# Moving batch 4's key-value product one unit later inside a hand-written order, and reordering tile 3 around it

## The chip, the cores and the metric

The kernel runs on one core of a Trainium2 chip. That core has a matrix engine (TensorE, PE in the profile, with its weight loads in a row of their own, PEld), a vector engine (VectorE, DVE), a scalar engine (ScalarE, ACT), a general engine (GpSimd, POOL) and a queue processor that issues most DMAs (SyncE, SP). Each engine works through its own instructions strictly in the order in which the program lists them, and waits on semaphores for what other engines have to deliver. The metric is the device time of one execution in microseconds; lower is better.

## The reference

Two things are computed one after the other, an efficient attention (softmax over the head dimension for the queries, over the sequence for the keys) and a two-layer network with a leaky ReLU:

```python
q_s = exp(q - max(q, axis=-1));  q_s /= sum(q_s, axis=-1)      # q, k, v: 8 x 8 x 576 x 64, float32
k_s = exp(k - max(k, axis=2));   k_s /= sum(k_s, axis=2)
kv  = einsum('bhsd,bhse->bhde', k_s, v)
x   = einsum('bhsd,bhde->bhse', q_s, kv)                       # then reshaped to 4608 x 512
h   = x @ w_in                                                 # 512 x 2048
out = maximum(0.01 * h, h) @ w_out                             # 2048 x 512 -> 4608 x 512
```

## The kernel before

Attention goes by batch (8 batches of 576 rows), the network by tile of 512 rows (9 tiles, numbered 0 to 8). The attention output is kept transposed in `xT`, which holds four batches and wraps round; tile 3 takes the last rows of batch 2 and the first 320 rows of batch 3, tile 4 the rest of batch 3 and the first 256 rows of batch 4. Matrix products run in bf16 with float32 sums. From tile 1 on the second layer, and from tile 5 on part of the first, is done with a seven-product scheme in place of eight (sums of blocks are formed on VectorE beforehand).

The order of the work is written out by hand. After the prologue, one long list of words, `SCORE`, is played word by word; each word emits a few instructions on one engine. So the list is at the same time the order of five in-order queues: where two words belong to different engines, only their dependencies bind them, and where they belong to one engine, the later one waits behind the earlier one. The words near the change, with `t` the tile and `b` the batch in the name:

- `tuij` is one unit of the first layer on TensorE: four matmuls of 128x512 into one PSUM bank (line 516; in tile 4, where the columns wrap round `xT`, eight of 128x256). A tile has 16 units, `u00` to `u07` and `u10` to `u17`. `tlij` is the leaky ReLU of that unit on ScalarE (line 525), which empties the bank into `gj`.
- `tPnsh` is a quarter of product `n` of the second layer on TensorE: four matmuls of 128x256 (line 947). Products 1, 6, 7 and 4 follow each other in one bank, 5 and 3 in a second, 2 in a third. `tn` are the block sums of `gj` on VectorE (`gs`, line 1004), on which products 5, 6, 7 and 3 depend. `tq1`, `tq5`, `tq6` and `tq21` copy a bank out on ScalarE before the next product goes on in it; `td11`, `td12` and `td22` are the closing sums on VectorE (line 896), and `tw` is the store of an output half, four DMAs on SP.
- For a batch `b`: `lk`, `lq`, `lv` load keys, queries and values (SP). `kt`, `km` and `ks` find the maximum of the keys and subtract it (VectorE; from batch 5 on the subtraction is on POOL, line 193); `ke` is their exponential (ScalarE, line 201) and `va`, `vb` cast the two halves of the values into `vb` (ScalarE, line 211). `kv` is the key-value product: 72 small matmuls on TensorE (line 294), into two PSUM banks for batch 4 and into the spare ends of two banks already taken for batches 5 to 7. `kr` (VectorE, line 326) and `kd` (ScalarE, line 332) divide it by the sum of the exponentials.
- `qm`, `qs`, `qe`, `qu`, `qn` are the softmax of the queries (VectorE, POOL line 256, ScalarE line 264, VectorE lines 273 to 275, VectorE line 280), and `qt` turns the result by a transposing DMA on SP into `qX` (line 457). `A` is the attention product of the turned queries on TensorE (line 438), `x` its copy into `xT` on ScalarE (line 429).
- `F` forms sums of `w_in` on VectorE that tile 5 needs (line 780), `X` sums of `xT`.

Buffers come from pools: six PSUM banks (`psB`) are shared by the first layer's units, product 2, the key-value product of batch 4 and the attention products (two banks each), two further banks (`psO`) by the other products. Six large buffers (`raw`) hold loaded keys, queries and values and later some sums. `vb` and `ke` exist once, so the casts and the exponential of batch 5 have to come after batch 4's key-value product has been computed; `gj` is a ring of five blocks.

What plays the list:

```python
def play(words, t=None):
    for word in words:
        if t is not None:
            of_tile(t, word)
        elif word[0].isdigit():
            of_tile(int(word[0]), word[1:])
        else:
            of_batch(word)
```

Of the kernel before, what the change touches and what calls it, by code (L numbers as in the profile page):

```python
# [25 lines left out]
def kernel(  # L26
# [17 lines left out]
    F2, O = moe_w_out.shape  # L44
# [741 lines left out]
    def xsums(t, steps=slice(0, 4)):  # L786
# [20 lines left out]
        qs3 qe3 2u14 2l14 2u02 2u06 2u12 lk5 2l05 2u13 2l02 2l06 2l12 km3 2u07 2u16 2u03 qu3 qn3 2l07 2l13  # L807
        2u17 1q21 2l03 2u15 2l15 2P100 ks3 ksB3 2n0_0 2l17 qs4 2P101 2P110 2P111 2P200 2l16 2P201 2P210
        2P211 2P500 2n0_1 2n1_0 2n1_1 2P501 2P510 lk4 kt4.0 lq5 ke3 kv3 kr3 2q1 2d11 2n2_0 1w0 2P600 qt3
        2P601 lv6 2P610 2P611 2P511 kd3 A3.0 kt4.1 2n2_1 2n3_0 kt4.2 2n3_1 A3.1 2q6 kt4.3 2q5 A3.2 2P700  # L810
        2P701 2P710 x3.01 2P711 x3.11 2d22 x3.10 2P300 x3.20 2P301 2P310 x3.21 qe4 km4 ks4 ksB4 kt5.0 lv4
        2P311 x3.00 2P400 va4 2P401 2P410 kt5.1 3u02 3l02 2P411 3u03 3u00 vb4 3l00 kt5.2 kt5.3 3u01 3l01 km5
        3l03 ke4 3u11 3l11 3u06 3u04 3l04 3u16 2q21 3l06 3l16 3u12 3l12 3u14 3u10 3l10 lk6 ks5 qu4 3u15 3l15
        kv4 3l14 kr4 kd4 3u07 2d12 qn4 3u05 3u13 3u17 3P100 3l05 3l07 3P101 3P110 3P111 lk7 3l13 3n0_0 3P500
        lv5 3l17 3n0_1 3P501 3P510 3q1 ke5 3n1_0 3n1_1 3n3_0 3P511 3P600 3n3_1 3q5 3P601 va5 3P610 3P611 3q6
        1w1 3P300 3P301 3P310 vb5 3P311 kt6.0 3n2_0 qt4 A4.0 A4.1 A4.2 kv5 x4.01 kt6.1 3n2_1 x4.00 x4.21
        x4.10 2w0 va6 3P700 kt6.2 kt6.3 3P701 3P710 qm5 qs5 3P711 3P200 3P201 x4.11 3P210 3P211 x4.20 kr5
        kd5 3d22 vb6 4u02 4l02 3P400 3P401 3d11 3P410 4u04 4u00 qe5 4l00 3P411 km6 4l04 4u05 4l05 3q21 4u03
        4u14 4l14 4l03 4u10 4l10 4u06 lv7 4u07 4u11 4l11 4u01 4l01 4l06 3d12 4l07 qu5 qn5 ks6 kt7.0 3w0 4u12
        4l12 4u13 F3 4l13 F1 4P100 4P101 4P110 F2 ke6 4u15 4P111 4q1 4n0_0 4l15 4u17 4l17 kt7.1 4n1_0 4u16  # L820
        3w1 4P500 4l16 4n0_1 4n2_0 qt5 A5.0 A5.1 x5.01 x5.10 x5.00 A5.2 kv6 x5.20 kt7.2 2w1 x5.11 4P501
        4P510 4n1_1 4P511 4q5 x5.21 4n3_0 4P600 4n3_1 4P200 4P601 4P610 4n2_1 X5.0 4P300 4P611 lq6 X5.1 X5.2
        4P201 4P301 4P310 4q6 X5.3 4P700 4P701 5u00 va7 kt7.3 4P210 F4 vb7 4P710 4P711 qm6 qs6 4d22 lq7 kr6
# [320 lines left out]
```

## Time and profile before

| | |
|---|---|
| median of 3 runs | 267.97 us (267.54 to 268.38) |
| the profiled execution | 267.58 us, of which the span of the instructions is 265.8 us |
| PE busy | 255.6 us (96%), 2570 instructions |
| DVE busy | 223.2 us (84%) |
| ACT busy | 193.7 us (73%) |
| POOL busy | 63.0 us (24%) |
| granted TensorE clock | 1.0 over the span |

A row of the chain or of a timeline gives start, duration and what ran, with `xN` for N instructions merged. In the chain of the work that ended last, "issue" is time for which the profile shows no cause. In the list of waits, a row says who waited for whom, for how long in total, how often, and the longest wait. A small share of matmul records can be missing from a trace, and the ends of matmuls are modelled. Tile 3's first layer runs from about 103 to 118 us, its second layer to about 134 us, tile 4's first layer from there to about 148 us.

### The profile page before, as it was taken

To read this page: it belongs to the slowest core of one execution; us is meant where nothing else is said; L and a number is where in the kernel's file an instruction comes from. 1 tells how busy PE (TensorE), PEld (TensorE's weight loads), DVE (VectorE), ACT (ScalarE), POOL (GpSimd) and SP (SyncE) were. 2 spreads that over 40 slices of the span, in tenths; PEclk is the share of its full clock that TensorE was granted. 3 is DMA by queue.
4 is the path that set the end of the run, shared out by engine and by line. 5 is a ranking of instruction groups with operands and counts; after the bars stand their busy time and mean duration, and the time that the engine had idled before them with its cause. 6 is when DMAs were issued, how large, how long until landed. Compare 5 with 4: busy or idle time off the path is not lost.

```text
span 265.8 us, 6314 instructions
## 1 busy us (share of the span) xinstructions
PE 255.6 (96%) x2570; PEld 190.1 (72%) x2582; DVE 223.2 (84%) x365; ACT 193.7 (73%) x370; POOL 63.0 (24%) x45
## 2 busy tenths in 40 slices
PE   8689999999999999999999999999999999999992
PEld 3267754457865687458888876688888888888882
DVE  2997899799998999989889896994998579679952
ACT  4977893699659769978887747887996489528930
POOL 2484442260038000250670019800000000000000
PEclk9999999999999999999999999999999999999999
DMA  7999999999898694858457725040382060042004
GB/s 241 344 210 357 317 210 273 337 310 294 250 397 298 149 327 143 289 221 176 174 129 155 225 72 170 18 91 4 85 176 68 21 139 2 0 97 63 1 2 158
DMA packets 37645, 46.48 MB, mean 175 GB/s; under 512 B 18160, under 2 KB 21232, under 8 KB 37616
## 3 DMA queue, kind: packets, MB, share of 16 engines
q1 hardware_dynamic: 32976, 36.64, 48.0%
q0 software_dynamic: 4320, 8.91, 13.4%
q10 hardware_dynamic: 320, 0.52, 0.6%
q8 instruction: 20, 0.33, 0.5%
q14 instruction: 9, 0.07, 0.1%
HBM read 36.70 MB, written 9.44 MB: 174 GB/s over the span
## 4 chain that ended last, share of the span: by engine, by line
PE 84%; DMA 6%; ACT 2%; DVE 1%; issue 1%; POOL 0%; ACTq 0%; POOLq 0%
PE acc L947 37%; PE ph L516 28%; PE ph L917 15%; DMA w_in_sb<-in_moe_w_in_dram 3%; DMA qX<-qe 3%; PE po L438 2%; PE pkv L294 1%; ACT ke L201 1%; PE po L294 1%; DVE k_raw L380 1%; PE pout L541 1%; ACT vb L211 1%; ACT qe L264 0%; POOL w_in_sb L129 0%; DVE out_sb L896 0%
## 5 line engine op out<-in xcount | busy, mean ns | idle before, releaser
L516 PE MATMUL ph<-xT,w_in_sb 128*128 128x256 bf16 (+3 forms) x488 | 83.6, 323 | 0.9 <-DMA w_in_sb<-in_moe_w_in_dram 0.2
L525 ACT ACTIVATE gj<-ph 128x512 bf16<-128x512 f32 (+2 forms) x113 | 59.1, 577 | 14.3 <-PE ph L516 11.1
L516 PEld LDWEIGHTS <-w_in_sb 128*128 128x128 bf16 x496 | 48.1, 98 | 29.6 <-DMA w_in_sb<-in_moe_w_in_dram 0.7
L947 PEld LDWEIGHTS <-gs 128*128 128x128 bf16 x512 | 49.5, 98 | 6.4 <-issue 0.2
L256 POOL TENSOR_TENSOR q_raw<-q_raw,qmax 128x2304 f32<-128x2304 f32 (+3 forms) x10 | 29.7, 2975 | 64.9 <-DVE qmax L225 64.9
L947 PEld LDWEIGHTS <-gj 128*128 128x128 bf16 x384 | 37.4, 98 | 6.8 <-issue 0.5
L947 PE MATMUL acc<-w_out_sb,gj 128*128 128x256 bf16 x256 | 32.4, 273 | 0.0
L947 PE MATMUL acc<-wsum,gs 128*128 128x256 bf16 x256 | 30.8, 273 | 0.0
L947 PE MATMUL acc<-w_out_sb,gs 128*128 128x256 bf16 x256 | 30.6, 273 | 0.0
L896 DVE TENSOR_TENSOR part_spare<-ph,part_spare 128x512 f32<-128x512 f32 x39 | 25.5, 684 | 3.4 <-PE ph L917 2.8
L981 ACT COPY part_spare<-ph 128x512 f32<-128x512 f32 x39 | 21.5, 594 | 8.7 <-PE ph L917 8.3
L429 ACT CAST xT<-po 128x512 bf16<-128x512 f32 (+3 forms) x47 | 19.0, 488 | 7.6 <-PE po L438 7.6
L1004 DVE TENSOR_TENSOR gs<-gj 128x1024 bf16<-128x1024 bf16 (+1 forms) x40 | 22.3, 577 | 2.0 <-ACT gj L525 2.0
L273 DVE TENSOR_REDUCE qsum<-qe 128x36 f32<-128x2304 bf16 (+4 forms) x11 | 19.7, 1793 | 3.3 <-ACT qe L264 3.3
L917 PEld LDWEIGHTS <-fs_spare 128*128 128x128 bf16 x208 | 20.3, 98 | 3.0
L280 DVE TENSOR_TENSOR qe<-qe,qrec 128x2304 bf16<-128x2304 bf16 (+4 forms) x12 | 22.1, 1842 | 0.3
L1004 DVE TENSOR_TENSOR gs<-gj,gs 128x1024 bf16<-128x1024 bf16 (+1 forms) x40 | 22.1, 578 | 0.3
L1014 ACT COPY keep<-acc 128x512 f32<-128x512 f32 x22 | 12.8, 587 | 12.1 <-PE acc L947 12.0
L193 POOL TENSOR_TENSOR k_raw<-k_raw,kall 128x2304 f32<-128x2304 f32 x3 | 15.2, 5074 | 26.7 <-ACT gj L525 25.9
L896 DVE TENSOR_TENSOR out_sb<-acc,keep 128x512 f32<-128x512 f32 (+1 forms) x26 | 16.6, 644 | 5.4 <-issue 2.8
L917 PE MATMUL ph<-xs_spare,fs_spare 128*128 128x256 bf16 x156 | 20.9, 273 | 0.0
L225 DVE TENSOR_REDUCE qmax<-q_raw 128x36 f32<-128x2304 f32 (+4 forms) x11 | 19.6, 1793 | 0.7 <-DMA q_raw<-in_q_dram 0.7
(89 smaller groups left out, 323.0 us busy)
## 6 DMA issues: line engine op xcount, KB each, us to landing
out_dram<-out_sb SPq DMA_DIRECT2D x68, 128.0 KB, 2.4
q_raw<-in_q_dram SPq DMA_DIRECT2D x6, 1152.0 KB, 6.2
v_raw<-in_v_dram SPq DMA_DIRECT2D x6, 1152.0 KB, 7.3
k_raw<-in_k_dram SPq DMA_DIRECT2D x5, 1152.0 KB, 8.8
w_in_sb<-in_moe_w_in_dram POOLq DMA_DIRECT2D x4, 512.0 KB, 7.9
w_out_sb<-in_moe_w_out_dram POOLq DMA_DIRECT2D x3, 512.0 KB, 16.0
k_raw<-in_k_dram SPq DMA_DIRECT2D x2, 576.0 KB, 5.4
v_raw<-in_v_dram SPq DMA_DIRECT2D x2, 576.0 KB, 7.3
```

What stands on the lines that cost most here:

```text
L225: nc.vector.tensor_reduce(out=m, in_=st[b]["q"][:, :, rs], axis=AX.X, op=ALU.max)
L256: eng.tensor_tensor(out=qs, in0=qs, in1=st[b]["qmax", rs.start].unsqueeze(3).to_broadcast([P, HL, n, D]), op=ALU.subtract,)
L273: nc.vector.reduce_sum(out=qsum, in_=st[b]["qe"][:, rs], axis=AX.X)
L280: eng.tensor_tensor(out=qes, in0=qes, in1=st[b]["qrec", rs.start].unsqueeze(3).to_broadcast([P, n, HL, D]), op=ALU.mult,)
L429: eng.copy(out=o, in_=i)
L516: nc.tensor.matmul(ph[:, n0:n1], lhsT=w_in_sb[:, i, j * P : (j + 1) * P], rhs=xT[:, i, (c0 + n0) % NX : (c0 + n0) % NX + n1 - n0], start=( ...
L525: nc.scalar.activation(out=o, in_=ph, func=AF.Prelu, alpha=LEAKY_SLOPE)
L896: nc.vector.tensor_tensor(out=o, in0=x, in1=y, op=ALU.add)
L917: nc.tensor.matmul(bank[x, t, p][:, jj], lhsT=lhs(k, 2 * p + jj), rhs=rhs[:, k], start=(first and k == 0 and jj == 0), stop=(k == 1), skip ...
L947: nc.tensor.matmul(b[:, at_], lhsT=lhs(k)[:, sub * P : (sub + 1) * P], rhs=rhs[:, k], start=(first and k == 0 and at_ == 0), stop=(k % (NK ...
L981: nc.scalar.copy(out=fill(t, kind, p), in_=bank["Z" if kind == "s5" else "X", t, p])
L1004: nc.vector.tensor_tensor(out=o, in0=x, in1=y, op=ALU.subtract)
```

## The change

Only the list of words changes; no word is added or taken away. The words from product 6 of tile 2 to the first block sums of tile 4 stand in a new order. `kv4` stands after 13 units of tile 3's first layer where it stood after 12. `2P411` comes before the first unit where it stood after it. The units, and with them the leaky ReLUs, of tiles 3 and 4 are permuted. `vb4` stands ahead of all of tile 3's leaky ReLUs, `va5` stands right behind `kv4` and ahead of four of them where it stood in the second layer. On VectorE `2d12` is taken ahead of `qu4`, `3d22` ahead of `kr5`, and `F1`, `F2` ahead of `kt7.0`. On SP the order `lv4 lk6 lk7 lv5 1w1 qt4 2w0 lv7 3w0` becomes `lv4 1w1 lv5 lk6 qt4 2w0 lv7 lk7 3w0`. POOL's order stays.

```diff
-        2P601 lv6 2P610 2P611 2P511 kd3 A3.0 kt4.1 2n2_1 2n3_0 kt4.2 2n3_1 A3.1 2q6 kt4.3 2q5 A3.2 2P700
-        2P701 2P710 x3.01 2P711 x3.11 2d22 x3.10 2P300 x3.20 2P301 2P310 x3.21 qe4 km4 ks4 ksB4 kt5.0 lv4
-        2P311 x3.00 2P400 va4 2P401 2P410 kt5.1 3u02 3l02 2P411 3u03 3u00 vb4 3l00 kt5.2 kt5.3 3u01 3l01 km5
-        3l03 ke4 3u11 3l11 3u06 3u04 3l04 3u16 2q21 3l06 3l16 3u12 3l12 3u14 3u10 3l10 lk6 ks5 qu4 3u15 3l15
-        kv4 3l14 kr4 kd4 3u07 2d12 qn4 3u05 3u13 3u17 3P100 3l05 3l07 3P101 3P110 3P111 lk7 3l13 3n0_0 3P500
-        lv5 3l17 3n0_1 3P501 3P510 3q1 ke5 3n1_0 3n1_1 3n3_0 3P511 3P600 3n3_1 3q5 3P601 va5 3P610 3P611 3q6
-        1w1 3P300 3P301 3P310 vb5 3P311 kt6.0 3n2_0 qt4 A4.0 A4.1 A4.2 kv5 x4.01 kt6.1 3n2_1 x4.00 x4.21
-        x4.10 2w0 va6 3P700 kt6.2 kt6.3 3P701 3P710 qm5 qs5 3P711 3P200 3P201 x4.11 3P210 3P211 x4.20 kr5
-        kd5 3d22 vb6 4u02 4l02 3P400 3P401 3d11 3P410 4u04 4u00 qe5 4l00 3P411 km6 4l04 4u05 4l05 3q21 4u03
-        4u14 4l14 4l03 4u10 4l10 4u06 lv7 4u07 4u11 4l11 4u01 4l01 4l06 3d12 4l07 qu5 qn5 ks6 kt7.0 3w0 4u12
-        4l12 4u13 F3 4l13 F1 4P100 4P101 4P110 F2 ke6 4u15 4P111 4q1 4n0_0 4l15 4u17 4l17 kt7.1 4n1_0 4u16
+        2P601 lv6 2P610 2P611 2P511 kd3 A3.0 kt4.1 2n2_1 2n3_0 kt4.2 A3.1 A3.2 2n3_1 2q6 2P700 2P701 2P710
+        2P711 kt4.3 2q5 2d22 km4 2P300 2P301 lv4 2P310 x3.21 1w1 x3.10 2P311 x3.00 2P400 2P401 x3.20 2P410
+        2P411 x3.11 x3.01 qe4 3u02 3u13 va4 vb4 lv5 3u04 3l04 3u15 3l15 3l02 3l13 3u00 3l00 3u10 ks4 ksB4
+        kt5.0 kt5.1 kt5.2 ke4 3u06 3l06 3u05 3l05 3u07 3l10 3u17 lk6 3l07 3l17 kt5.3 km5 ks5 3u03 2d12 3u01
+        3l01 3u14 3l03 qu4 2q21 kv4 va5 kr4 3l14 3u11 qn4 3u12 3l12 3l11 3u16 3l16 3P100 3P101 3P110 3n0_0
+        kd4 3P111 3P500 3n0_1 3q1 3n1_0 3n1_1 3n3_0 3P501 3P510 3P511 3P600 3P601 3P610 ke5 3P611 3q5 3n3_1
+        kt6.0 3n2_0 vb5 3P300 3P301 3P310 3P311 qt4 kt6.1 kt6.2 3q6 3n2_1 A4.0 A4.1 kt6.3 A4.2 x4.00 kv5
+        3P700 3P701 3P710 3P711 x4.10 va6 3P200 x4.20 qm5 3d22 3P201 x4.21 2w0 3P210 3P211 x4.11 x4.01 4u00
+        kr5 3P400 3P401 3P410 kd5 3P411 lv7 4u06 4l00 vb6 lk7 4u01 3d11 3q21 qs5 qe5 4u07 4l06 4l01 km6 ks6
+        4u03 4u02 4l02 4l03 4u04 4l04 3d12 3w0 qu5 qn5 4l07 4u05 4l05 4u13 4P100 4P101 4P110 4l13 F1 F2 4u10
+        ke6 kt7.0 4u14 4u11 4l11 4u12 4u15 4l10 F3 4l12 4l15 4n0_0 4P111 4q1 4l14 4u17 4l17 kt7.1 4n1_0 4u16
```

## The prediction, made before the changed kernel ran

> **What bounds the kernel now.** I read the profile's page first, then the list of TensorE's own waits, then the chain of work that ended last around tile 3. The page:
>
> ```profile
> PE 255.6 (96%) x2570; PEld 190.1 (72%) x2582; DVE 223.2 (84%) x365; ACT 193.7 (73%) x370; POOL 63.0 (24%) x45
> PE   8689999999999999999999999999999999999992
> ```
>
> TensorE is busy 255.6 of 265.8 us, and the row of slices shows that the rest lies in the first slices and the last. From 48 to 261 us the list of waits has one entry for TensorE:
>
> ```profile
> PE po L438 <- DMA qX<-qe: 0.3, 1, 0.3
> ```
>
> It belongs to the turned queries of batch 1, before the region that changes. So in tile 3 TensorE waits for nothing; the chain there:
>
> ```profile
> 103.49 0.21 PE ph L516
> ...
> 104.35 0.44 PE acc L947 x4
> 104.79 9.28 PE ph L516 x43
> 114.07 0.15 issue
> 114.22 0.78 PE pkv L294 x72
> ...
> 118.56 6.99 PE acc L947 x64
> 125.54 0.62 PE po L438 x16
> ...
> 130.43 0.87 PE ph L516 x8
> ...
> 147.90 0.44 PE acc L947 x4
> ```
>
> These rows give the prices on TensorE: a unit of tile 3 costs 0.86 us (103.49 to 104.35, its four matmuls), a quarter product 6.99/16 = 0.44 us, batch 4's key-value product 0.78 us. The only row that looks like a hole in front of that product is the 0.15 us "issue". But the 43 matmuls before it stand for eleven units, which are 44: at 0.86/4 = 0.215 us each, 44 take 9.46 us, and 104.79 + 9.46 = 114.25 us, where the product starts. A record is missing; there is no hole. The work on TensorE is the same set in both orders, so from 103.49 to 147.90 us there is nothing to win beyond the fractions of 0.1 us that stay unexplained, and the question is only whether the new order makes TensorE wait.
>
> **The change part by part.** I lay the new order of TensorE out at these prices and ask of each hand-over what is ready when. I take the old clock throughout, as nothing before 103.49 us moves on TensorE.
>
> **First layer of tile 3 on TensorE.** `2P411` now comes first (103.49 to 103.93), then thirteen units to 103.93 + 13 x 0.86 = 115.1, then the key-value product to 115.9, and three units to 118.56, the old end. The product is 0.86 us later than before, by the one unit.
>
> **ScalarE around it.** Its rows of before:
>
> ```profile
> 100.48 2.20 ACT L264 ACTIVATE qe<-q_raw 128x2304 bf16<-128x2304 f32 x1
> 102.81 1.23 ACT L211 CAST vb<-v_raw 128x1152 bf16<-128x1152 f32 x1
> 104.88 1.15 ACT L211 CAST vb<-v_raw 128x1152 bf16<-128x1152 f32 x1
> 108.39 2.13 ACT L201 ACTIVATE ke<-k_raw 128x2304 bf16<-128x2304 f32 x1
> ...
> 128.62 0.79 ACT L429 CAST xT<-po 128x512 bf16<-128x512 f32 x2
> 132.78 2.13 ACT L264 ACTIVATE qe<-q_raw 128x2304 bf16<-128x2304 f32 x1 [0.68 <-POOL q_raw L256]
> 141.82 2.56 ACT L525 ACTIVATE gj<-ph 128x512 bf16<-128x512 f32 x5 [0.28 <-PE ph L516]
> 144.22 2.16 ACT L201 ACTIVATE ke<-k_raw 128x2304 bf16<-128x2304 f32 x1
> ```
>
> A leaky ReLU costs (144.22 - 141.82)/5 = 0.48 us of queue. `qe4` starts 0.3 us later than 100.48, as `x3.00` is now ahead of it; `va4` and `vb4` follow without a gap and end at 105.0 us. The first leaky ReLU, `3l04`, waits for its unit (103.93 + 3 x 0.86 = 106.5), so nothing is lost by the cast in front of it. From there: `3l04` 106.55, `3l15` 107.4, `3l02`, `3l13`, `3l00` to 109.4, `ke4` to 111.4, then `3l06`, `3l05`, `3l10`, `3l07`, `3l17` at 0.48 each, the last done at 113.9. With six banks, the first six units start freely; later ones need banks given back. If a bank goes to the next user in the order in which banks were given back, the seventh unit (109.1) needs `3l04` (done 107.2), the twelfth (113.4) needs `3l06` (112.0), and the product (115.1) the banks of `3l10` and `3l07` (113.4). The smallest margin is 1.4 us. The raw buffers are given out that way:
>
> ```profile
> 91.96 2.27 SPq L83 DMA_DIRECT2D v_raw<-in_v_dram  x2
> 102.70 3.72 SPq L83 DMA_DIRECT2D k_raw<-in_k_dram  x2
> 110.54 0.37 SPq L83 DMA_DIRECT2D v_raw<-in_v_dram  x1
> 110.96 3.34 SPq L754 DMA_DIRECT2D out_dram<-out_sb  x4
> 118.83 2.69 SPq L457 DMA_TRANSPOSE qX<-qe  x1
> v_raw<-in_v_dram SPq DMA_DIRECT2D x1, 1152.0 KB, 8.1
> v_raw<-in_v_dram SPq DMA_DIRECT2D x1, 1152.0 KB, 6.4
> ```
>
> `lk6` starts at 102.70, right when `qe4` ends (100.48 + 2.20), `lv5` at 110.54, right when `ke4` ends (108.39 + 2.13): each takes the oldest buffer given back.
>
> **SP.** `1w1` moves ahead of `lv5` and `lk6`, to about 94.3 us, behind `lv4`. Its sums are long ready, so it doesn't hold the queue. `lv5` then takes the queries' buffer at the end of `qe4` (103.0) and lands, at 6.4 us, at 109.5; `lk6` takes the values' buffer at 105.0. `lk7` moves behind `lv7`, to about 125 us, and is first read by `kt7.0` beyond 140 us. Batch 4's values, issued at 93.86 (the end of the first row less its issue of 0.37), landed 8.1 us later, at 102.0, 0.8 us ahead of `va4`. The store's 4 x 128 KB come right behind. At the rate of these rows (2304 KB from 91.96 to 102.0, 230 KB per us) they cost at most 2.2 us if they share the engines evenly, nothing if they stay behind; I take nothing, as the load is first in the same queue. With 2.2 us the casts end at 107.2 to 107.4 and `3l04` is done at 108.0, still ahead of the seventh unit at 109.1. The Trainium skill (DMA: Bandwidth & Descriptors, "Issuing engines are not separate DMA queues") says that all DMAs run on the same 16 engines and interleave, which speaks against moving the store up; by it the sum would take the 2.2 us, and the end would still not move. No trace here shows these two side by side.
>
> **Behind the product.** `va5` waits for the product to have read `vb`, so it runs from 115.95 to 117.0, ahead of `3l14`, `3l12`, `3l11`, `3l16` and `kd4`. `3l12` waits for its unit (117.7) anyway and `3l16` for the last unit (118.56); the four end by 118.3, 118.8 and 119.3. What it takes away comes back later: before, `va5` stood in the second layer. VectorE and POOL:
>
> ```profile
> 86.53 2.56 DVE L280 TENSOR_TENSOR qe<-qe,qrec 128x2304 bf16<-128x2304 bf16 x1
> 115.20 0.67 DVE L896 TENSOR_TENSOR out_sb<-acc,keep 128x512 f32<-128x512 f32 x1
> 115.79 2.98 DVE L280 TENSOR_TENSOR qe<-qe,qrec 128x2304 bf16<-128x2304 bf16 x1
> 118.69 1.28 DVE L1004 TENSOR_TENSOR gs<-gj 128x1024 bf16<-128x1024 bf16 x2
> 134.94 2.55 DVE L273 TENSOR_REDUCE qsum<-qe 128x36 f32<-128x2304 bf16 x1 [0.96 <-ACT qe L264]
> 137.94 3.08 DVE L280 TENSOR_TENSOR qe<-qe,qrec 128x2304 bf16<-128x2304 bf16 x1
> 145.60 0.68 DVE L1004 TENSOR_TENSOR gs<-gj 128x1024 bf16<-128x1024 bf16 x1
> 111.27 5.07 POOL L193 TENSOR_TENSOR k_raw<-k_raw,kall 128x2304 f32<-128x2304 f32 x1 [25.92 <-ACT gj L525]
> 133.54 5.07 POOL L193 TENSOR_TENSOR k_raw<-k_raw,kall 128x2304 f32<-128x2304 f32 x1 [0.79 <-issue]
> ```
>
> The product is 0.86 later, but `2d12` (0.59 us of queue, 115.79 - 115.20) is now ahead of it in VectorE's idle time, so `qn4` starts 0.27 later, at 116.06. It took 2.56 us alone and 2.98 and 3.08 where POOL's subtraction still ran for 0.55 and 0.67 us, so the later start may cost nothing: it ends between 118.77 (2.4 after POOL's end at 116.34, as both rows do) and 119.04. `3n0_0` and `3n0_1` then end by 120.24 at the latest; they need `3l11` (118.8) and `3l16` (119.3). Their users `3P500` and `3P501` start at 118.56 + 4 x 0.44 = 120.3 and 120.75. Margin 0.5 us or more; cost zero. `3q1` and all behind it hang on TensorE's own time and stay.
>
> **The turn of batch 4.** `qt4` is issued behind `qn4`, at 118.83 to 119.1. `A4.0` needs it at 125.54. The landings between 85 and 150 us, then of all nine turns:
>
> ```profile
> DMA to landing us min/median/max: 4.6/4.6/6.3
> ...
> DMA to landing us min/median/max: 3.1/4.6/7.6
> ```
>
> The 6.3 us is this very turn, so it landed at 125.1 with 0.4 us to spare. The new turn has the same DMAs around it and lands between 123.4 and 125.4. Cost zero, with 0.1 us left at the bad end.
>
> **Tile 4.** The copies of `A4` end about where they did (129.4); the first unit, now `4u00`, comes at 130.4. `qe5` stands behind `3q21` now, which waits for the last quarter of product 4 at 133.05, so `qe5` goes from 132.78 to 133.6, and `qu5` and `qn5` follow 0.8 later (135.75, 138.75). `qn5` then starts after POOL's end at 138.61 and takes 2.56, so it ends at 141.3 against 141.02; with 3.08, at 141.8. Its turn lands at 146 to 148.1, needed at 148.3. `F1`, `F2`, `kt7.0`, `F3` are the same work, so `4n0_0` ends at 146.5 to 147.0, needed at 147.90. The leaky ReLUs behind `qe5`: `4l05` done at 140.0, needed by `4P101` at 140.46; banks there have over 1 us. Cost zero. From `4u16` on the order is the old one.
>
> **The sum** is zero: 267.58 us for the profiled execution, which is 265.8 us of span and 1.78 around it. It lies 0.39 below the median of the runs, 267.97, and I predict 268.0 us. What the measurement can tell from no change is about 0.3%, 0.8 us.
>
> **The rivals.**
>
> Slower, by a late turn: the turned queries of batch 4 (or, after the later `qn5`, of batch 5) land after TensorE wants them, and as TensorE has no slack every part of it is lost. At the trace's longest landing of 7.6 us the turn lands at 119.1 + 7.6 = 126.7, 1.16 us after 125.54, and the time is 269.1 us. It decides from a landing of 7.3 us on (0.8 us lost). For it speaks that this turn was slow before; against it that 1152 KB of loads and the store `1w1` are out of its way now. Chance 0.11.
>
> Slower, by ScalarE behind the product: if `va5` is late by d (batch 5's values not landed, or the casts slower), `3l16` and `3n0_1` are late with it; TensorE begins to lose at d = 0.7 us and has lost 0.8 at d = 1.5. The values would have to land at 117.5 for that, 14.5 us after the issue, against 6.4 measured. A hand-over of banks in another order than assumed would do the same: if the seventh unit got the sixth one's bank, it would wait from 109.1 to 112.9, 3.8 us, 271.8 us. Both and whatever I have overlooked: 0.16.
>
> Faster: TensorE isn't at its limit, and the new mix gets more out of it.
>
> ```profile
> 110.00:120.00 10.00, 9.80 (x121) 5.46 (x122) 8.81 (x14) 8.12 (x18) 5.07 (x1) 1.00 0.60 205
> 130.00:140.00 10.00, 10.00 (x94) 8.96 (x93) 8.59 (x14) 7.74 (x13) 7.82 (x2) 1.00 0.41 96
> ```
>
> Weight loads are busy 5.46 us of ten in tile 3's first layer and 8.96 in tile 4's. If that share were the limit, the 64 matmuls of tile 3's layer could go at tile 4's pitch (0.87/8 = 0.109 us), and 64 x (0.215 - 0.109) = 6.8 us would be free, 261.2 us. Against it: tile 4's matmuls are 256 columns wide at 0.109 us and tile 3's 512 wide at 0.215, so each moves the same columns per us at a granted clock of 1.00, and the pitch goes by width, not by loads. The Trainium skill (Perfetto Trace Analysis, "Identifying the Most-Contended Engine") calls matmul busy time a bad measure and names the share of weight loads as the better one; here the pitch decides against it. What is left is under 0.5 us of pieces, which stays within 0.3%. Chance of more than that: 0.03.
>
> **How the numbers follow.** The forecast of no change has 0.70, in 267.2 to 268.8 (0.3% either side). The late turn has 0.11 (to 269.1), the other losses 0.16, faster 0.03. A range from 267.2 to 269.1 takes in the forecast and most of the late turn, about 0.8, and leaves out the larger losses and the gain.
>
> **What would show it.** Right: the list of waits of TensorE has no new entry; tile 3's `3P100` starts at 118.5 or so and the quarter product behind `4u16` at 147.9; the key-value product starts at 115.1, `qn4` ends by 119.04, batch 4's turn lands before 125.5. Wrong: an idle time of TensorE ahead of line 438 at 125.5 or 148 (the turn), ahead of line 947 at 120 (ScalarE or VectorE), or ahead of line 516 between 109 and 118 (banks).

## The result and the profile after

The changed kernel takes 268.69 us (median of 9 runs, 268.13 to 268.82) against 267.93 us (267.54 to 268.40), a ratio of 1.0023 with a 95% interval of 1.0015 to 1.0032. It is slower by 0.76 us between the medians, 0.6 us by the ratio. That lies in the forecast range and under the 0.3% that counted there as no change, but it is clear of zero, and zero was the sum.

The page of the changed kernel, which has the same TensorE time as before to the tenth, in a span 1.1 us longer:

```profile
span 266.9 us, 6318 instructions
PE 255.6 (96%) x2571; PEld 190.1 (71%) x2582; DVE 222.5 (83%) x365; ACT 193.6 (73%) x370; POOL 63.0 (24%) x45
```

TensorE's list of waits from 48 us on has one row, as before, but it counts two waits where it counted one:

```profile
PE po L438 <- DMA qX<-qe: 0.5, 2, 0.3
```

The chain of the changed kernel, at the places shown of before and at the second wait:

```profile
98.70 5.35 PE acc L947 x48
104.05 0.43 PE ph L516 x2
104.48 0.05 issue
104.53 10.74 PE ph L516 x49
115.27 0.74 PE pkv L294 x72
...
118.70 6.99 PE acc L947 x64
125.69 0.62 PE po L438 x16
...
148.07 0.44 PE acc L947 x4
...
174.95 6.43 DMA qX<-qe
181.38 0.04 issue
181.42 0.69 PE po L438 x16
```

The reordered stretch is not where the time went. Against before (98.58, 118.56, 125.54, 147.90) the changed kernel is late by 0.12 us already where the stretch begins (as it is by 0.14 us at TensorE's first unit at 23 us, long before any word that moved), and by 0.17 where it ends: 0.05 us for the whole new order. The two other rises come behind it, where no word was moved. At 181 us TensorE starts the attention product of batch 6, 0.45 later than before (180.97), so 0.28 is lost on the turned queries of batch 6; before, that turn landed in 4.7 us:

```profile
qX<-qe SPq DMA_TRANSPOSE x1, 4.7
```

The last 0.65 us is lost after TensorE has finished. From its last matmul to the end of the span it takes 4.70 us before and 5.35 after, and in that time nothing runs but VectorE's last closing sum (0.42 us) and the last stores.

### The profile page after: what moved, and what is told of

Its sections match the earlier page's. It is cut to its first block, busy times and chain, and to the rows that moved or that the text cites. A ratio compares the mean times of both kernels' runs of the same rounds, so it can differ in the third digit from the quotient of the medians.

```text
span 266.9 us, 6318 instructions
## 1 busy us (share of the span) xinstructions
PE 255.6 (96%) x2571; PEld 190.1 (71%) x2582; DVE 222.5 (83%) x365; ACT 193.6 (73%) x370; POOL 63.0 (24%) x45
## 4 chain that ended last, share of the span: by engine, by line
PE 80%; DMA 9%; ACT 3%; DVE 1%; issue 1%; POOL 0%; DVEq 0%; ACTq 0%; POOLq 0%
PE acc L947 34%; PE ph L516 27%; PE ph L917 15%; DMA qX<-qe 5%; DMA w_in_sb<-in_moe_w_in_dram 3%; PE po L438 2%; ACT gj L525 1%; PE pkv L294 1%; ACT ke L201 1%; PE po L294 1%; DVE k_raw L380 1%; PE pout L541 1%; ACT vb L211 1%; DVE part_spare L896 1%; ACT qe L264 0%
## 5 line engine op out<-in xcount | busy, mean ns | idle before, releaser
L280 DVE TENSOR_TENSOR qe<-qe,qrec 128x2304 bf16<-128x2304 bf16 (+4 forms) x12 | 21.4, 1780 | 0.3
```

The lines of the kernel that those rows point to most:

```text
L280: eng.tensor_tensor(out=qes, in0=qes, in1=st[b]["qrec", rs.start].unsqueeze(3).to_broadcast([P, n, HL, D]), op=ALU.mult,)
```

## The experiments

Each timed run was compared with the kernel before on the same chip. The columns: the distance of the attention products of batch 3 and batch 5 on TensorE, which spans the reordered words; that from batch 5's to batch 6's; how long batch 6's turn took to land; the tail, from the end of the last matmul to the end of the span; all four from one trace each. Then the median and the ratio with its interval.

| kernel | 3 to 5 | 5 to 6 | turn of 6 | tail | median us | ratio |
|---|---|---|---|---|---|---|
| before | 50.36 | 32.71 | 4.67 | 4.70 | 267.93 | |
| before, again | 50.37 | 32.71 | 4.63 | 4.68 | 267.59 | 0.9998 (0.9989 to 1.0007) |
| after | 50.42 | 32.98 | 6.43 | 5.35 | 268.69 | 1.0023 (1.0015 to 1.0032) |
| after, again | 50.42 | 32.71 | 4.63 | 5.34 | 268.23 | 1.0018 (1.0008 to 1.0027) |
| first half of the change | 50.39 | 32.80 | 6.24 | 5.39 | 268.21 | 1.0021 (1.0012 to 1.0030) |
| second half | 50.39 | 32.72 | 4.64 | 4.70 | 267.66 | 1.0003 (0.9994 to 1.0011) |
| before, 1 more on VectorE | 50.37 | 32.82 | 6.26 | 5.39 | 268.29 | 1.0020 (1.0010 to 1.0030) |
| before, 1 more on POOL | 50.36 | 32.72 | 4.63 | 4.94 | 267.98 | 1.0001 (0.9993 to 1.0010) |
| after, 8 more on VectorE | 50.41 | 32.84 | 6.28 | 4.92 | 268.24 | 1.0016 (1.0006 to 1.0026) |
| after, 8 more on POOL | 50.42 | 32.73 | 6.18 | 4.68 | 268.12 | 1.0011 (1.0002 to 1.0019) |
| after, one pair put back | 50.42 | 32.83 | 6.28 | 4.63 | 267.85 | 1.0005 (0.9997 to 1.0014) |
| after, 4d12 later | 50.42 | 32.97 | 4.65 | 5.36 | 268.81 | 1.0035 (1.0022 to 1.0048) |
| after, both of these | 50.42 | 32.97 | 4.64 | 4.64 | 268.12 | 1.0009 (1.0001 to 1.0018) |
| before, kv4 alone | 50.47 | 32.78 | 6.22 | 4.65 | 267.90 | 1.0009 (0.9999 to 1.0019) |

**The two kernels again, and the two halves of the change.** The halves cut the list behind `3P311`. The first has the new order up to there and then what is left of the old one, the second the reverse:

```diff
-   old ... 3P311 | kt6.0 3n2_0 qt4 A4.0 A4.1 A4.2 kv5 ... (old)
+   new ... 3P311 | lk7 3q6 qt4 A4.0 A4.1 A4.2 kv5 x4.01 ... (first half: old from here)
+   old ... 3P311 | kt6.0 3n2_0 qt4 kt6.1 kt6.2 3n2_1 A4.0 ... (second half: new from here)
```

> The kernel before, unchanged, against itself, to see what one execution's trace has by chance. If the 0.76 us between the medians sit where the two traces differ (batch 6's turn, +0.27 us of TensorE around 171 to 182 us, and the last stores, +0.65 us from the end of TensorE to the end of the span) and come from an instruction fetch that falls on a DMA engine just then, this trace may show one or the other of them in a part of its executions: the ratio is 1.000 within 0.1%, TensorE's quarter product behind 4u16 starts 49.3 us after the one at 98.6. If the loss is made in tile 3, this trace has neither.

> The changed kernel once more. Theory of the fetches: the ratio is again 1.002 to 1.003; the stretch from the quarter products at 98.7 us to the one behind 4u16 takes 49.3 to 49.4 us as in both traces; what is lost lies behind it, at batch 6's turn (a wait of TensorE on the turned queries of 0.1 to 0.3 us) and in the last stores (over 5.2 us from TensorE's end to the end of the span against 4.7). Theory of the region: that stretch is longer by up to 0.7 us in some executions and the tail is not.

> The new order up to the end of product 3 of tile 3, the old one behind it. Theory of the region: the loss is made where the order changed, so this half or the other has most of the 0.7 us, and the two add up to it. Theory of the fetches: nothing is lost in the region; each half comes out at 267.9 or near 268.7 as its own instruction counts and offsets decide, the two need not add up, and where time is lost, it is behind 170 us.

> The old order up to the end of product 3 of tile 3, the new one behind it. Theory of the region: it has what the first half does not have of the 0.7 us, to be seen between 125 and 148 us. Theory of the fetches: the stretch up to 148 us is as long as in the kernel before, within 0.1 us; a loss, if there is one, lies behind 170 us.

The reordered stretch costs the same 0.06 us in both traces of the changed kernel and about half of it in each half, so the theory that the loss is made there falls. In these six traces the tail falls into two kinds with nothing between: 4.68 and 4.70 in before (twice) and the second half, 5.34 to 5.39 in after (twice) and the first half. So the tail comes with the first half of the change. The late turn is something else: it is in one trace of the changed kernel and not in the other, so it can come and go with the same program.

What the tails differ in stands in the DMA view. From 262 to 268 us, first before and then after (40 slices of 0.15 us; below them the landings of the stores issued in the window):

```profile
GB/s 232 287 259 328 287 328 314 287 314 355 369 396 314 178 14 0 0 0 0 0 0 0 0 0 0 0 0 55 0 0 0 0 0 0 0 0 0 0 0 0
...
out_dram<-out_sb SPq DMA_DIRECT2D x1, 128.0 KB, 2.7
out_dram<-out_sb ACTq DMA_DIRECT2D x1, 128.0 KB, 3.0
```

```profile
GB/s 424 382 151 246 246 328 314 314 328 314 273 287 273 396 451 287 178 27 14 0 27 27 14 0 0 0 0 0 0 0 0 0 0 0 0 0 0 0 0 0
...
q14 instruction: 1, 0.01, 0.3%
...
out_dram<-out_sb SPq DMA_DIRECT2D x1, 128.0 KB, 3.6
out_dram<-out_sb ACTq DMA_DIRECT2D x1, 128.0 KB, 3.9
```

Before, the stores run out at 264.3 us, and a single transfer of 55 GB/s stands by itself at 266.1. That is an instruction fetch of 8 KB, and by then the kernel is over. After, the fetch is at 264.2, among the stores, and behind it the transfer thins out to 14 to 27 GB/s, a few packets at a time, for 0.9 us. These last packets follow one another singly, as if one DMA engine alone still had to write; the trace does not name the engines. The two last stores land in 3.6 and 3.9 us where they took 2.7 and 3.0. The fetch stands alone in a window of 0.4 us of before (266 to 266.4 us), and beside the stores in one of after (264 to 264.4 us):

```profile
q14 instruction: 1, 0.01, 8.0%
```

```profile
q10 hardware_dynamic: 53, 0.10, 63.8%
q1 hardware_dynamic: 32, 0.04, 27.9%
q14 instruction: 1, 0.01, 4.8%
```

The Trainium skill (Runtime: NRT & Kernel Launch, "Instruction fetch mechanics") says that each engine's instructions are streamed in by DMA in blocks of 16 KB while it runs, at a cost mostly hidden; here the fetches are of 16 KB on one queue but of 8 KB on the other, and this one goes with a tail 0.65 us longer. By the same skill (DMA: Bandwidth & Descriptors, "Queues, rings and completion order") a DMA engine takes turns between the queues that have work for it; the trace, which names no engine, agrees as far as the last packets come singly behind the fetch.

**Whose fetch it is.** The traces with the long tail so far have one instruction more on VectorE and one more on POOL than the others, both of them semaphore waits, which stand in front of an instruction that has more to wait for. On VectorE they are at these lines, before and then after:

```profile
L896 DVEq EVENT_SEMAPHORE  x59: 21/49/5264, 74.3 to 258.3; - x59
L326 DVEq EVENT_SEMAPHORE  x2: 21/21/21, 126.9 to 182.4; - x2
L225 DVEq EVENT_SEMAPHORE  x1: 21/21/21, 74.8 to 74.8; - x1
```

```profile
L896 DVEq EVENT_SEMAPHORE  x60: 21/50/5265, 74.4 to 258.8; - x60
L326 DVEq EVENT_SEMAPHORE  x1: 21/21/21, 182.8 to 182.8; - x1
L225 DVEq EVENT_SEMAPHORE  x2: 21/21/21, 74.9 to 125.5; - x2
```

With `3d22` ahead of `kr5` the wait stands in front of `3d22` (one more at 896, one fewer at 326), which alone adds nothing: the second half of the change has this swap, with 60, 1 and 1 of them, and the short tail. `qm5` waits for one thing more (225), and that is the one more in all: the first half has 59, 2 and 2, without the swap, and the long tail. Whether such an instruction is enough was tried with empty ones, put where the engine still waits for its first load; the computation is unchanged:

```diff
     nc.gpsimd.memset(vb[:, :, :, D : D + 1], 1.0)
+    spacer = const_pool.tile([P, 1], FP32, name="spacer")
+    for _ in range(1):                      # 1 on before, 8 on after
+        nc.vector.memset(spacer, 0.0)       # or nc.gpsimd
```

> The kernel before with one empty instruction more on VectorE (a one-element-wide memset while it still waits for its first load). The long tails so far (5.34 to 5.39 us from TensorE's end to the end of the span, against 4.68 to 4.70) stand in the traces with one instruction more on VectorE and on POOL, and in them an 8 KB instruction fetch falls into the last stores. If it is VectorE's fetch that one instruction moves, this kernel gets the long tail and 0.5 to 0.7 us with it, with the whole order of before; if it is POOL's, its tail stays at 4.7 us and its time at the one of before.

> The kernel before with one empty instruction more on POOL, at the same place. The reverse of the one on VectorE: a tail of 5.3 to 5.4 us and 0.5 to 0.7 us more if it is POOL's fetch, 4.7 us and no change if it is VectorE's. If neither of the two lengthens the tail, the count of instructions isn't what places the fetch.

> The changed kernel with eight empty instructions more on VectorE at the start. If VectorE's fetch makes the long tail, eight instructions earlier it falls before the last stores are issued (before 259 us), the tail goes back to 4.7 us, and the time comes down by 0.5 to 0.7 us, to within 0.1% of the kernel before, with the new order as it is. If it is POOL's, the tail stays at 5.3 us. If the loss were one of the new order, nothing would come back.

> The changed kernel with eight empty instructions more on POOL at the start. If POOL's fetch makes the long tail, it moves to the middle of the kernel (POOL's last eight instructions before the end begin before 165 us), the tail goes back to 4.7 us and 0.5 to 0.7 us come back; if it is VectorE's, nothing changes: a tail of 5.3 us and a ratio to before of 1.002.

One empty instruction on VectorE makes the kernel before as slow as the changed one, 1.0020 against 1.0018 to 1.0023, with the whole old order: tail 5.39 us, and the fetch at 264.0 among the stores. One on POOL doesn't (1.0001; its fetch stays behind the end), though its tail is 4.94 us and not the 4.7 expected: its last two stores land 0.2 to 0.3 us later than before, with no fetch beside them, and the trace shows no reason. So it is VectorE's list that brings the long tail. The trace itself names the queue of the fetch and not the engine that it is for.

The two kernels with eight more did not come out as expected. Eight more on VectorE move the fetch to 259.57 us, ahead of the last stores, of which the first is issued at 260.20. The tail shortens only to 4.92, and the time doesn't come back clearly (1.0016), where I had expected 4.7 us and 0.1% of before. The fetch is not among the stores there. What is different is that VectorE begins its closing sums at 258.88, 2.61 us ahead of TensorE's end, where it is 2.96 before and after, and that the last store is issued 0.85 us behind that end where it is 0.50; why VectorE is late is not shown. Eight more on POOL were to change nothing if the fetch is VectorE's, and that failed too: the fetch comes at 263.56, 1.9 us behind the last matmul where in the long tails it is 2.6 to 2.7 behind, the tail is 4.68, as was expected if the fetch were POOL's, and the ratio is 1.0011. So POOL's list bears on the fetch as well, in a way that these runs do not show. A fetch among the stores isn't enough for a long tail; it depends on when it comes, and on which of the DMA engines it runs I could not see.

**Undoing one pair, and moving the turn.** Two edits to the changed kernel, alone and together. The first puts `3d22` behind `kr5` again, which takes one wait out of VectorE's list. The second takes `4d12` behind `qn6`, meant to issue batch 6's turn earlier:

```diff
-   ... x4.20 qm5 3d22 3P201 x4.21 2w0 3P210 3P211 x4.11 x4.01 4u00 kr5 3P400 ...
+   ... x4.20 qm5 3P201 x4.21 2w0 3P210 3P211 x4.11 x4.01 4u00 kr5 3d22 3P400 ...
```

```diff
-   ... 5c11_3 qs7 4d12 5u01 ... 5l10 5l13 5u14 qn6 5P110 ...
+   ... 5c11_3 qs7 5u01 ... 5l10 5l13 5u14 qn6 4d12 5P110 ...
```

> The changed kernel with one pair put back on VectorE: 3d22 behind kr5, as before. That takes one semaphore wait out of VectorE's list, so it has as many instructions as in the kernel before. Theory of VectorE's fetch: the fetch falls behind the last stores again (266 us), the tail is 4.7 us, and 0.4 to 0.6 us come back; what is left over before is the 0.05 us of the region and the hits on batch 6's turn (0 to 0.3 us), a ratio of 1.000 to 1.001. If the new order itself cost the time, one pair could not give it back.

> The changed kernel with 4d12 taken behind qn6 on VectorE, so that batch 6's turn is issued 0.7 us earlier, near 174.3 us. Theory of the hits: its data are all written by 178.6 us, before TensorE's own instruction fetch at 179.3 to 179.5 us, the turn lands in 4.6 us, and TensorE does not wait for it. The tail stays at 5.3 to 5.4 us, so of the 0.5 to 0.8 us only the hits (0 to 0.3 us) come back: a ratio of 1.0010 to 1.0018. If the turn is late for another reason, it still takes over 6 us in the trace.

> Both together: the new order without the late fetch and without the hit. A tail of 4.7 us, a turn of batch 6 of 4.6 us, a ratio of 1.000 to 1.0005; it can beat the kernel before only by what the hits cost that one on average, under 0.1 us.

Putting the pair back gives back all that can be measured: 267.85 us, the median of before, a ratio of 1.0005 whose interval holds 1. The tail is 4.63 us, and the fetch is behind the end again, at 266.4. Its windows from 262 to 268 and from 266.3 to 266.7 us:

```profile
out_dram<-out_sb SPq DMA_DIRECT2D x1, 128.0 KB, 2.6
out_dram<-out_sb ACTq DMA_DIRECT2D x1, 128.0 KB, 3.0
...
q14 instruction: 1, 0.01, 4.8%
```

All else of the new order, the later key-value product with it, is still there, and so is the one wait more on POOL (29 where before has 28). On VectorE the three lines now have 59, 1 and 2 waits: the one that `qm5` added stays, and the edit took another away, so that the list has 81 in all as before, against 82 after. The tail is short in all traces with 81 and no empty instruction (4.63 to 4.70 us), and long in all with 82 and none (5.34 to 5.39), whichever wait it is. So the 0.65 us go with the number of instructions on VectorE, and not with the order of the work.

The second edit did not do what it was for: 1.0035 was measured where 1.0010 to 1.0018 was expected, and 1.0009 where 1.000 to 1.0005 was, with the pair put back. `4d12` had stood in a wait: the next sums on VectorE (`5c12_3`) wait for TensorE in any case, so `qn6` did not come earlier, and the turn was issued 26.51 us behind batch 5's product as in before. All that the edit did was to put the 0.6 us of `4d12` in front of the block sums of tile 5. The chain of that kernel shows TensorE waiting for them:

```profile
172.74 2.46 DVE qe L280
175.21 0.60 DVE out_sb L895
175.81 0.61 DVE gs L1003
176.42 0.05 issue
176.46 5.41 PE acc L946 x48
```

This costs 0.26 us (32.97 against 32.71), alone and with the pair put back. With the 0.06 for the stretch and the 0.66 for the tail it makes 0.98 us, 0.37%, and 0.35% was measured; as this trace loses 0.28 us more at a turn of batch 2, the match is in part luck.

The turn itself was late, at 6.2 to 6.4 us to land, in seven of the fourteen traces, and early, at 4.6 to 4.7, in the other seven; old and new order stand on both sides. In the changed kernel's trace its packets run at their usual 205 to 221 GB/s and end at 179.3 us, then 16 KB of instructions stand alone for 0.92 us, and as they end, at 180.3, two last packets of 4 bytes come. The DMA view from 179.2 to 180.4 us, before and then after, and of after from 180 us on:

```profile
q8 instruction: 1, 0.02, 4.9%
```

```profile
q8 instruction: 1, 0.02, 4.8%
q1 hardware_dynamic: 5, 0.00, 0.5%
```

```profile
q1 hardware_dynamic: 2, 0.00, 0.7%
```

Before, all packets of the turn are through by 179.2 us. After, three of the five are its last data, and the two others stand behind the fetch; the turn counts as landed 1.1 us after them. It costs TensorE between 0.02 and 0.28 us. In the seven early traces the fetch starts 0.2 to 0.4 us behind the turn's last packet, in the seven late ones within 0.1 us of its last data, so small shifts decide it. That a shift of the fetch makes the turn late wasn't tried by itself, as the edit for it moved nothing.

Other turns show the same. Batch 4's takes 6.2 to 6.4 us in all fourteen traces, of the old order and the new, and in each a fetch of 16 KB starts within 0.02 us of its last data (at 123.08 us in the trace of before). The second turn of batch 2 takes 4.9 us in place of 3.1 to 3.2 in three traces (after again, eight more on POOL, `4d12` later), each time with such a fetch at its end, and TensorE loses 0.17 to 0.35 us there, ahead of all words that moved.

**The title alone.** `kv4` one unit later in the kernel before, the rest as it was:

```diff
-   ... 3u15 3l15 kv4 3l14 kr4 kd4 3u07 2d12 qn4 ...
+   ... 3u15 3l15 3u07 kv4 3l14 kr4 kd4 2d12 qn4 ...
```

> The kernel before with nothing but batch 4's key-value product one unit later (behind 3u07), the counts of instructions as before. By the reading that no wait stands in front of the product, nothing is won: qn4 and the turn of batch 4 are 0.6 to 0.9 us later, the turn lands at 125.2 to 125.9 us against the 125.5 us at which TensorE wants it, so TensorE loses 0 to 0.4 us there; tail 4.7 us. Ratio 1.000 to 1.0015. If the 0.15 us in front of the product were a wait, 0.1 us would come back there.

There was nothing to win in front of the product: 50.47 us against 50.36 for the stretch, 0.1 us more. The ratio's interval reaches from 0.9999 to 1.0019. Most of the 0.1 us stands behind the turn of batch 4, which lands at 125.33 where TensorE then starts at 125.37:

```profile
118.34 6.99 PE acc L946 x64
125.33 0.04 issue
125.37 0.69 PE po L438 x16
```

No version beat the kernel before.

## Why the prediction was right, and what it missed

**What bounds the kernel: right.** TensorE has no slack from 48 to 261 us, the 0.15 us ahead of the product was a missing record, and nothing could be won. In the second trace of before, which has all 44 records, there is no such row:

```profile
104.79 9.50 PE ph L516 x44
114.29 0.71 PE pkv L294 x72
```

The kernel with `kv4` alone later won nothing there, and the stretch costs the same or more in every variant.

**The hand-overs in the stretch: right, nearly to the tenth.** The rows of the changed kernel that answer to the forecast, from ScalarE, VectorE and SP (0.1 us must be taken off for the late start):

```profile
106.68 0.60 ACT L525 ACTIVATE gj<-ph 128x512 bf16<-128x512 f32 x1 [1.43 <-PE ph L516]
109.46 2.15 ACT L201 ACTIVATE ke<-k_raw 128x2304 bf16<-128x2304 f32 x1
115.88 1.18 ACT L211 CAST vb<-v_raw 128x1152 bf16<-128x1152 f32 x1
116.21 2.67 DVE L280 TENSOR_TENSOR qe<-qe,qrec 128x2304 bf16<-128x2304 bf16 x1
119.00 1.29 DVE L1004 TENSOR_TENSOR gs<-gj 128x1024 bf16<-128x1024 bf16 x2
103.19 0.37 SPq L83 DMA_DIRECT2D v_raw<-in_v_dram  x1
105.28 0.37 SPq L83 DMA_DIRECT2D k_raw<-in_k_dram  x1
118.94 2.71 SPq L457 DMA_TRANSPOSE qX<-qe  x1
```

`3l04` was forecast at 106.55, `ke4` at 109.4, `va5` at 115.95, `qn4` at 116.06 with an end between 118.77 and 119.04 (it took 2.67 us and ended at 118.88), `lv5` at 103.0, `lk6` at 105.0 and the turn at 118.8 to 119.1. The two loads went to the buffers named. The values of batch 4 landed at 102.80 instead of 101.98 with the store behind them, so of the 2.2 us that sharing the engines could have cost, 0.7 to 0.8 came about, and the cast was not held up. The turn landed at 125.3 us, 0.4 ahead of its use, at the late end of what was forecast.

**The sum: zero was wrong, and the range held by luck.** The 268.69 us lie in it because 0.3% either side is wider than the loss, not because the loss was foreseen. "From `4u16` on the order is the old one", the last step ahead of the sum, was true and was taken to mean that nothing would change there. Two things did. The tail grew by 0.65 us, since the reorder added one semaphore wait to VectorE's list, and with it the last instruction fetch came among the last stores and not behind the end. I counted words and their times, but not the waits that come with a new order, and had no term for the fetch at all. And TensorE can wait for the turn of batch 6, by 0.28 us in the profiled execution; there is no such step in the forecast, and of its signs of being right the first, no new wait of TensorE, failed by it.

**The rivals.** The late turn came in kind, though at batch 6, not at 4 or 5, and with a fetch of 16 KB and not with loads; its size stayed under 0.3 us where 0.8 was put as the point of decision. The 6.3 us of batch 4's turn were read without their cause, and it was held against the rival that loads and the store `1w1` are out of its way now. Before, these had all landed by 118.28 us, ahead of its issue at 118.83; it goes with a fetch in both orders, and took 6.26 us before and 6.38 after. ScalarE behind the product and the banks cost nothing. That TensorE had room left by the share of its weight loads showed nowhere: its busy time is 255.6 us in both orders.

## What to carry to other kernels

Where an engine has no idle time and its work stays the same, a reorder has nothing to win on it, and what it loses may lie far from the words that moved: compare the two traces by distances between fixed points first, and the tail after the last compute instruction with them. Count instructions and not only work, as a wait more is an instruction more, and with one more on VectorE the last fetch fell elsewhere. A difference of 0.2% between two orders may say nothing of the orders: one empty instruction in the old one made the same difference, and swapping two words back in the new one took it away.

## What was not expected of the hardware

An instruction fetch of 8 KB among the last stores, 2.6 to 2.7 us behind the last matmul, lengthened the tail by 0.65 to 0.7 us in all five traces that have it there (after twice, the first half, one more on VectorE, `4d12` later); at 1.9 us behind the tail was the short one, though the last two stores still took 3.0 and 3.2 us to land. What sets the moment of the fetch, and why the earlier one does so little, stays open. So do the tails of 4.92 and 4.94 us, which have no fetch among the last stores. The kernel with eight more on POOL is at 1.0011 with a short tail; its trace is 0.28 us late at 48 us already and loses 0.17 at the second turn of batch 2, and whether that is what the ratio holds is not shown.
